# Twelve tiles of T written out in groups of five over six steps, and used again as raw weight tiles

## The chip, the cores and the metric

One Trainium2 chip; the kernel runs on one of its cores. The metric is the device time of one execution in microseconds (us), median of several executions. The kernel before took 1963.73 us (median of 3, 1962.33 to 1965.15).

## The reference

What is computed is one block with two branches on a sequence of 8192 rows of 448 channels. The first branch is a spectral mixer: layer norm, a Fourier transform over the 8192 rows, a small two-layer complex network on the frequencies in 4 blocks of 112 channels, and the inverse transform. The second is a gated feed-forward layer (GEGLU) of width 1792.

```python
mod = (_silu(c) @ w_mod).reshape(c.shape[0], 6, 1, -1)
sa, ca, ga, sb, cb, gb = (mod[:, 0], ..., mod[:, 5])
h = _layernorm(x, axis=-1) * (1 + ca) + sa
x = x + ga * _A_ref(h, A_w1, A_b1, A_w2, A_b2)      # rfft2, MLP, soft threshold, irfft2
h = _layernorm(x, axis=-1) * (1 + cb) + sb
x = x + gb * _B_ref(h, B_w_gate, B_w_up, B_w_down)  # (gelu(x@w_gate) * (x@w_up)) @ w_down
return x
```

## The kernel before

**Three stages.** The 8192 rows are taken as 128 x 64. In the first stage (0 to about 70 us) the 16 chunks of x are loaded into 16 tiles `xbuf[0..15]` (128 x 4 x 448, fp32), normalized and transformed over the 128 (`dft_a`, L198, line 200); the result T overwrites the chunk. In the second stage (70 to about 395 us) T is transformed over the 64, sent through the network and back. The third stage, to the end, does the last inverse step and the whole feed-forward layer; it is almost all matmuls.

**T goes through DRAM.** The second stage needs T with its rows arranged differently, so T is written to the DRAM tensor `td` and read back. T's 128 rows lie in an order in which every fourth partition belongs to one quarter: `store_t(ch, c)` (L258, DMA in line 261) writes quarter c of chunk ch, 32 partitions of 1792 numbers, 224 KB. Chunks 0 to 3 are written whole in the first stage, and so is quarter 0 of the other twelve (`CE` = 4 to 15). What is left is 3 quarters x 12 chunks = 36 stores of 224 KB. Quarter 0 serves units 0 to 7 of the second stage, quarter 1 units 8 to 15, quarter 2 units 16 to 23, quarter 3 the last eight.

**Units and steps.** The second stage has 32 units, one half of the channels (h) by one set of frequencies (bt) each, in a software pipeline. `step(i)` (L524) does, in the order of the code:
- `fetch_t` of unit i+2 (L316): two DMAs `tr<-td` of 224 KB (line 319) into a tile `tr` that has two buffers, and for every second unit a table `s<-cs` of 256 KB (line 325);
- the hooks "load" and "pe": other work that is hung on this step by `at(i, hook, ...)`, such as the weights' norm pass;
- `stage_s2` of unit i (L342): 24 short matmuls `ps<-s,th/tl` (lines 351 to 353), their results taken by ACT (`zh`, line 359) and DVE (`zl`, line 360);
- `split_t` of unit i+1 (L332): ACT casts `tr` to `th`, then POOL (DVE for units 0 and 1) makes `tl` of the difference (both by the helper `split`, lines 105 and 107);
- `stage_m2` of unit i-2 (L431, matmuls in lines 424 to 429, ACT `t`, eight DVE operations `y`), `stage_i1` of unit i-3 (L468, matmuls in lines 477 to 479, two DMAs `vd<-us` in line 487), `stage_m1` of unit i-1 (L380, matmuls in lines 397 to 402, ACT `hh`, DVE `hl`).

**What sets the order.** The whole stage is under a manual schedule: each engine runs its instructions in the order of the code. All these DMAs are issued by SP, one after the other; SP stops at the first whose semaphores are not yet there, and each DMA also waits for the one issued eight before it, so that at most eight are under way.

**Where the stores stand.** Twelve (quarter 1) follow the fetch of unit 1 (L583), twelve (quarter 2) stand behind `step(0)`, twelve (quarter 3) behind `step(1)` (L594 to L597). Then the pool `qp`, which holds the twelve tiles, is closed (L598).

**The norm pass.** From step 3 on, the feed-forward weights are loaded once to find their norms: `load_w` (three DMAs, 512 KB, lines 657 and 659), `load_m` (448 KB, line 767), `load_mod_row` (two DMAs of 392 KB, line 628). Their raw tiles come from `npool`, eight in rotation (`raw_tile`, L615), in memory that `qp` has given back.

Of the kernel before, what the change touches and what calls it, by code (L numbers as in the profile page):

```python
# [10 lines left out]
F32 = mybir.dt.float32  # L11
# [10 lines left out]
NA, NB, NG = 128, 64, 64  # L22
# [7 lines left out]
NC = 4  # L30
CE = 4
# [14 lines left out]
def spectral_geglu(ctx, tc, x, w1, b1, w2, b2, wg, wu, wd, cvec, wmod, cf1, cs2, cmi, cgm, out):  # L46
# [85 lines left out]
    qctx = ExitStack()  # L132
    qp = qctx.enter_context(tc.tile_pool(name="qp", bufs=1))
    with ExitStack() as actx:
# [5 lines left out]
        xbuf = [(ap if i < CE else qp).tile([128, 4, D], F32, name=f"xt{i}") for i in range(NB // 4)]  # L140
# [17 lines left out]
        q, y, t, nm, mu = (ap.tile([128, NB], F32, name=nm) for nm in ("q", "y", "t", "nm", "mu"))  # L158
# [99 lines left out]
        def store_t(ch, c=None):  # L258

            r = slice(0, 128) if c is None else slice(c, 128, NC)  # L260
            dma(td[r, ch * 4 : ch * 4 + 4], xts[ch][r])
# [10 lines left out]
        for g, bs in enumerate(groups):  # L272
# [5 lines left out]
            at = [pos[0] + 0.06] + [pos[i] + d for i in (1, 2, 3) for d in (0.03, 0.06)] + [pos[3] + 0.1]  # L278
            if g == 0:
                at = [t_stats[e] + 0.2] + [pos[0] + 0.03] * 7  # L280
# [23 lines left out]
    with ExitStack() as bctx:  # L304
# [11 lines left out]
        def fetch_t(h, bt):  # L316
            raw = bp1.tile([128, GB, HC], F32, tag="tr", name="tr", bufs=2)
            for ri in range(2):
                dma(
                    raw[ri * 64 : ri * 64 + 64],  # L320
                    td[rows(ri, bt), :, h * HC : (h + 1) * HC].rearrange("g b c -> b g c"),
                )
            if (h, bt) not in s2s:
                s2 = bp1.tile([128, GB, 2, 128], F16, tag="s2", name="s2", bufs=2)
                dma(s2, cs2[:, bt * GB : (bt + 1) * GB])
                if (0, bt) in units[:NS]:

                    s2s[(1, bt)] = s2
                s2s[(h, bt)] = s2
            trs[(h, bt)] = raw, s2s.pop((h, bt))  # L330

        def split_t(h, bt, el=G):  # L332
            raw, s2 = trs.pop((h, bt))
            th = bp1.tile([128, GB, HC], F16, tag="th", name="th", bufs=2)
            tl = bp1.tile([128, GB, HC], F16, tag="tl", name="tl", bufs=2)
            split(th, tl, raw, el=el)
            tts[(h, bt)] = th, tl, s2

        cnt = {"z": 0, "h": 0}
        ctx_u = {}  # L340

        def stage_s2(h, bt):  # L342
# [88 lines left out]
        def stage_m2(h, bt, p):  # L431
            hs = ctx_u[("h", h, bt)]
            ps = bank("pc", "pm2")
            for kk in range(2):
                mlp2(ps[:, kk * HC : (kk + 1) * HC], hs, kk, 2 * h + kk, slice(p * 128, p * 128 + 128))
            t = bp.tile([128, D], F32, tag="t", name="t", bufs=2)

            S.activation(t, ps[:, :D], AF.Relu, bias=nlam)  # L438
            drip()
            y = bp.tile([128, 2, 2, BS], F32, tag="y", name="y", bufs=2)  # L440
            pv = ps[:, :D].rearrange("p (k r c) -> p r k c", k=2, r=2)
            tv = t.rearrange("p (k r c) -> p r k c", k=2, r=2)
            for gi in range(2):
                for ri in range(2):
                    si = slice(gi * 64, gi * 64 + 64)
                    V.scalar_tensor_tensor(  # L446
                        y[ri * 64 : ri * 64 + 64, gi], pv[si, ri], LAM, tv[si, ri], op0=ALU.add, op1=ALU.min
                    )
            drip()
            if bt == 0 and p == 0:  # L450

                pn = bank("pb", "pn")
                for kk in range(2):
                    mlp2(pn[:2, kk * HC : (kk + 1) * HC], hs, kk, 2 * h + kk, slice(ZW - 2, ZW))
                tn = bp.tile([2, D], F32, tag="t", name="tn", bufs=2)
                V.tensor_scalar(tn, pn[:2, :D], LAM, -LAM, op0=ALU.min, op1=ALU.max)
                pnv = pn[:, :D].rearrange("p (k r c) -> p r k c", k=2, r=2)
                tnv = tn.rearrange("p (k r c) -> p r k c", k=2, r=2)
                V.tensor_tensor(y[64:65, 0], pnv[0:1, 0], tnv[0:1, 0], ALU.subtract)
            return y.rearrange("p g k c -> p g (k c)")  # L460

        def split_y(y, el=G):
            yh = bp.tile([128, 2, HC], F32R, tag="yh", name="yh", bufs=4)
            yl = bp.tile([128, 2, HC], F32R, tag="yl", name="yl", bufs=4)
            split(yh, yl, y, el=el)
            return yh, yl

        def stage_i1(h, bt):  # L468
            ys = ctx_u.pop(("y", h, bt))
            us = bp.tile([128, GB, HC], F32, tag="us", name="us", bufs=2)  # L470
            for p in range(GB // 2):
                yh, yl = ys[p]
                ps = bank("pd", "pi1")
                parts = [(0, 0, 1), (1, 1, 2)] if bt == 0 and p == 0 else [(1, 0, 2)]
                for m, lo, hi in parts:
                    o = ps[:, lo * HC : hi * HC]
                    T.matmul(o, mih[:, m, :], yh[:, lo:hi], start=True, stop=False)
                    T.matmul(o, mih[:, m, :], yl[:, lo:hi], start=False, stop=False)
                    T.matmul(o, mil[:, m, :], yh[:, lo:hi], start=False, stop=True)
                out = riders.pop()(ps) if riders and p else None  # L480
                S.copy(us[:, 2 * p : 2 * p + 2, :], ps[:, :D].rearrange("p (g c) -> p g c", g=2))
                if out:
                    out()
            if (h, bt) in units[-2:]:
                to_v(bt, us)
            for ro in range(2):
                dma(
                    vd[h, :, ro * 64 + bt * GB : ro * 64 + (bt + 1) * GB],
                    us[ro * 64 : ro * 64 + 64],
                )  # L490
# [30 lines left out]
        def at(i, hook, fn, *args):  # L521
            side.setdefault((i, hook), []).append((fn, args))

        def step(i):  # L524
            def hook(name):
                for fn, args in side.get((i, name), []):
                    fn(*args)

            if i + 2 < nu:
                fetch_t(*units[i + 2])  # L530
            hook("load")
            hook("pe")
            if i < nu:
                stage_s2(*units[i])
            if i + 1 < nu:
                split_t(*units[i + 1], el=V if i < 1 else G)
            hook("act")
            m2 = 0 <= i - 2 < nu
            if m2:
                y0 = stage_m2(*units[i - 2], 0)  # L540
                y = stage_m2(*units[i - 2], 1)
                ys = [split_y(y0)]
            if 0 <= i - 3 < nu:
                stage_i1(*units[i - 3])
            if m2:
                ctx_u[("y",) + units[i - 2]] = ys + [split_y(y)]
                del ctx_u[("h",) + units[i - 2]]
            hook("dve")
            if 0 <= i - 1 < nu:
                stage_m1(*units[i - 1])  # L550
            hook("pool")
# [28 lines left out]
        mod_row0(1)  # L580
        mod_row0(0)
        fetch_t(*units[1])
        for ch in range(CE, NB // 4):  # L583
            store_t(ch, 1)

        zh = [bp1.tile([113, 2, ZW], F32R, name=f"zh{i}") for i in range(4)]
        hh_ = [bp1.tile([113, 2, ZW], F32R, name=f"hh{i}") for i in range(4)]
# [3 lines left out]
        split_t(*units[0], el=V)  # L591
        lctx.close()
        bp = bctx.enter_context(tc.tile_pool(name="bp", bufs=1, side="right"))
        for i in range(2):  # L594
            step(i)
            for ch in range(CE, NB // 4):
                store_t(ch, 2 + i)  # L597
        qctx.close()  # L598


        def pow2(s, bnd, p=15):

# [10 lines left out]
            raws[key] = fn(pool, *args)  # L613

        def raw_tile(pool):  # L615
            return pool.tile([128, 4, 256], F32, tag="raw", name="raw", bufs=8 if pool is npool else 4)

        def load_mod_row(pool, q):
            out = []
            for hh in range(2):  # L620
                if pool is None:
                    wm = bp1.tile([128, GB, HC], F32, tag="tr", name="tr", bufs=2)[:112]
                elif callable(pool):
                    wm = pool().rearrange("p q c -> p (q c)")[:112, : 4 * HC].rearrange("p (q c) -> p q c", q=4)
                else:
                    wm = raw_tile(pool)[:112, :, :HC]
                c0 = q * D + hh * HC
                dma(wm, wmod[:, c0 : c0 + HC].rearrange("(k p) c -> p k c", p=112))
                out.append(wm)
            return out  # L630
# [160 lines left out]
        npool = nctx.enter_context(tc.tile_pool(name="npool", bufs=1))  # L791
# [15 lines left out]
        at(11, "dve", row_scales)  # L807
        at(16, "pe", scales1)
        at(16, "pe", scales2)
        for i in range(2, 17):  # L810
            step(i)
        nctx.close()

        wpool = ctx.enter_context(tc.tile_pool(name="wpool", bufs=1))
        wh = wpool.tile([128, 4, 2 * F], F16, name="wh")
# [513 lines left out]
```

## Time and profile before

| | |
|---|---|
| median of the runs | 1963.73 us |
| the profiled execution, own time | 1967.95 us |
| its span on the core | 1966.2 us |
| mean granted TensorE clock | 0.988 |
| busy: PE / DVE / ACT / POOL | 98% / 56% / 40% / 59% |
| DMA, mean over the span | 83 GB/s |

One slice of the page's second part is 49 us. The first five slices moved 347, 293, 246, 238 and 221 GB/s, the slices from the eleventh on some 43 GB/s: transfers are heavy in the first two stages and light afterwards. The row of the granted clock has 9s throughout but for an 8 in the second and third slices and around the start of the third stage.

In the rows of a timeline the first two numbers are the start and the duration in us, a bracket at the end is the idle time of the engine before the instruction and who ended it. "SPq" is SP's queue: the duration of a row there is that of the issuing, not of the transfer.

### The profile page before, as it was taken

The page shows a single profiled execution, that of the slowest core. Times are in us where ns is not written, and L with a number is a line of the kernel's source. Part 1 is how long each engine was busy: PE and PEld are TensorE (multiplying, and loading weights), DVE is VectorE, ACT ScalarE, POOL GpSimd, SP SyncE. Part 2 cuts the span into 40 slices and gives each one's busy share as a digit, 9 for nine tenths or more (in the row PEclk, how much of TensorE's full clock was granted, in tenths as well). Part 3 has the DMA queues.
Part 4 walks back from the last instruction along what each step waited for, and adds up shares of the span by engine and source line. Part 5 has one row for each costly group of instructions (what it writes and reads, how often), then busy time and mean ns, then how long its engine had stood idle before and what let it go on. Part 6 is the DMA issues. An engine that isn't in the chain of part 4 may idle for free.

```text
span 1966.2 us, 43631 instructions
## 1 busy us (share of the span) xinstructions
PE 1921.5 (98%) x17668; PEld 1707.7 (87%) x17668; DVE 1105.6 (56%) x2340; ACT 792.6 (40%) x1345; POOL 1163.0 (59%) x1470
## 2 busy tenths in 40 slices
PE   7899999889999999999999999999999999999998
PEld 3599999778888988888888888888889888888898
DVE  8557788775555555555555555555555555555533
ACT  5567888643233333333333333333333333333322
POOL 3146755345666666666666666666666666666644
PEclk9889999989999999999999999999999999999999
DMA  9888867642111111111111111111111111111000
GB/s 347 293 246 238 221 181 200 160 143 64 43 43 43 43 49 46 43 43 43 42 43 43 42 43 43 43 44 43 43 44 43 43 44 43 44 43 43 22 16 20
DMA packets 168750, 163.35 MB, mean 83 GB/s; under 512 B 87328, under 2 KB 147364, under 8 KB 168548
## 3 DMA queue, kind: packets, MB, share of 16 engines
q1 hardware_dynamic: 168532, 160.56, 28.3%
q8 instruction: 138, 2.26, 0.5%
q14 instruction: 64, 0.52, 0.1%
q10 hardware_dynamic: 16, 0.01, 0.0%
HBM read 97.47 MB, written 47.25 MB: 74 GB/s over the span
## 4 chain that ended last, share of the span: by engine, by line
PE 85%; DVE 5%; ACT 4%; issue 2%; DMA 2%; POOL 1%; SPq 1%; ACTq 0%; DVEq 0%; POOLq 0%
PE pgu L1051 51%; PE pdn L1119 8%; PE pdn L1117 8%; PE pdn L1118 8%; DVE y L446 3%; PE ps L200 2%; PE pi L951 1%; ACT th L105 1%; ACT zh L359 1%; ACT hh L414 1%; DMA tr<-td 1%; PE psm L636 1%; ACT t L438 1%; PE pi L949 1%; PE pi L950 1%
## 5 line engine op out<-in xcount | busy, mean ns | idle before, releaser
L1051 PE MATMUL pgu<-nt,wh 128*128 128x256 f16 x6272 | 836.2, 274 | 0.0
L1051 PEld LDWEIGHTS <-wh 128*128 128x128 f16 x6272 | 603.8, 98 | 99.3 <-issue 30.7
L1087 ACT ACTIVATE gel<-pgu,dg 128x256 f32<-128x256 f32 x448 | 200.2, 472 | 799.8 <-PE pgu L1051 762.7
L1051 PE MATMUL pgu<-nt,wl 128*128 128x256 f16 (+1 forms) x3584 | 503.4, 273 | 6.0 <-ACT nt L1044 3.2
L1119 PE MATMUL pdn<-wd,ac 128*128 128x224 f16 x1568 | 406.1, 259 | 0.2 <-DVE ac L1110 0.2
L1117 PE MATMUL pdn<-wd,ac 128*128 128x224 f16 x1568 | 406.1, 259 | 0.0
L1118 PE MATMUL pdn<-wd,ac 128*128 128x224 f16 x1568 | 406.1, 259 | 0.0
L1098 POOL TENSOR_TENSOR x<-x 128x128 f32<-128x128 f32 x223 | 240.7, 1079 | 266.8 <-DVE x L1092 266.8
L1110 DVE SCALAR_TENSOR_TENSOR ac<-x,sa_act,ac 128x896 f16<-128x896 f32 (+1 forms) x225 | 308.2, 1370 | 83.6 <-ACT ac L1109 83.6
L1051 PEld LDWEIGHTS <-wl 128*128 128x128 f16 (+1 forms) x3584 | 298.4, 97 | 63.9 <-issue 30.1
L1092 DVE TENSOR_TENSOR x<-pgu,gel 128x256 f32<-128x256 f32 x448 | 179.5, 418 | 283.4 <-ACT gel L1087 282.7
L1109 ACT ACTIVATE ac<-x,sa_act 128x896 f16<-128x896 f32 (+1 forms) x225 | 232.9, 1035 | 53.3 <-POOL x L1101 51.2
L1154 POOL TENSOR_TENSOR o<-u,p 128x224 f32<-128x224 f32 x32 | 21.1, 660 | 292.1 <-DVE u L1153 292.1
L1099 POOL TENSOR_TENSOR x<-x 128x128 f32<-128x128 f32 x223 | 158.5, 711 | 17.5
L1119 PEld LDWEIGHTS <-ac 128*128 128x128 f16 x1568 | 153.4, 98 | 0.5 <-DVE ac L1110 0.5
L1117 PEld LDWEIGHTS <-ac 128*128 128x128 f16 x1568 | 153.4, 98 | 0.4
L1118 PEld LDWEIGHTS <-ac 128*128 128x128 f16 x1568 | 153.4, 98 | 0.4
L446 DVE SCALAR_TENSOR_TENSOR y<-pm,t 64x224 f32<-64x224 f32 x256 | 99.5, 389 | 48.0 <-ACT t L438 44.0
L107 POOL TENSOR_TENSOR yl<-y,yh 128x448 fp32r<-128x448 f32 x63 | 78.8, 1251 | 77.5 <-ACT yh L105 66.5
L1100 POOL TENSOR_TENSOR x<-x 128x128 f32<-128x128 f32 x223 | 114.1, 512 | 0.0
L1101 POOL TENSOR_TENSOR x<-x 128x128 f32<-128x128 f32 x223 | 108.3, 486 | 0.0
L107 POOL TENSOR_TENSOR tl<-tr,th 128x896 f16<-128x896 f32 x30 | 57.2, 1908 | 78.0 <-ACT th L105 75.7
(281 smaller groups left out, 2761.5 us busy)
## 6 DMA issues: line engine op xcount, KB each, us to landing
tr<-td SPq DMA_DIRECT2D x64, 224.0 KB, 4.2
vd<-us SPq DMA_DIRECT2D x64, 224.0 KB, 3.1
xx<-in_A_x SPq DMA_DIRECT2D x32, 448.0 KB, 3.3
v<-vd SPq DMA_DIRECT2D x63, 224.0 KB, 2.9
out<-x SPq DMA_DIRECT2D x31, 448.0 KB, 2.9
xt<-in_A_x SPq DMA_DIRECT2D x15, 896.0 KB, 13.4
td<-xt SPq DMA_DIRECT2D x48, 224.0 KB, 3.8
nt<-pk SPq DMA_TRANSPOSE x480, 2.3
```

The source lines that it names most:

```text
L107: (el or V).tensor_tensor(lo, src, h, ALU.subtract)
L446: V.scalar_tensor_tensor(y[ri * 64 : ri * 64 + 64, gi], pv[si, ri], LAM, tv[si, ri], op0=ALU.add, op1=ALU.min)
L1051: T.matmul(pgu[i, t, q][:, pr * H : (pr + 1) * H], w[rows, tw, f0 : f0 + 128], nts[i][rows, tn, :], start=start, stop=stop, skip_group_che ...
L1087: S.activation(gl, ps[:, :H], AF.Gelu_apprx_tanh, scale=dg)
L1092: V.tensor_tensor(dst, ps[:, H : 2 * H].rearrange("p (b c) -> p b c", b=2), gl.rearrange("p (b c) -> p b c", b=2), ALU.mult)
L1098: e.tensor_tensor(s1, a21, a22, ALU.add)
L1099: e.tensor_tensor(s2, s1, a11, ALU.subtract)
L1109: S.activation(ac[:, 0, k], x[:, k], AF.Copy, scale=sc)
L1110: V.scalar_tensor_tensor(ac[:, 1, k], x[:, k], sc, ac[:, 0, k], op0=ALU.mult, op1=ALU.subtract)
L1117: T.matmul(ps, ac[:, 0, ka], wds[t][:, 0, kb], start=t == 0, stop=False)
L1118: T.matmul(ps, ac[:, 0, ka], wds[t][:, 1, kb], start=False, stop=False)
L1119: T.matmul(ps, ac[:, 1, ka], wds[t][:, 0, kb], start=False, stop=t == NP - 1)
```

## The change

The 36 stores are put into one list, chunk by chunk: quarters 1, 2 and 3 of chunk 4, then of chunk 5, and so on. Six of them are issued behind the fetch of unit 1. Of the other thirty, five are hung on each of the steps 0 to 5, as the last of the hook "load", behind the step's fetch and behind the loads of the norm pass. A chunk is done when its third quarter is written, so that its tile is free for other use early; the raw tiles of the norm pass are now views of the tiles `xbuf[4..11]` (the first 1024 of their 1792 columns), eight in rotation as before. The pool `qp` stays open until the norm pass is over.

```diff
-        for ch in range(CE, NB // 4):
-            store_t(ch, 1)
+
+        late = [(ch, c) for ch in range(CE, NB // 4) for c in range(1, NC)]
+
+        def store_late(n):
+            for ch, c in late[:n]:
+                store_t(ch, c)
+            del late[:n]
+
+        store_late(6)
...
-        for i in range(2):
-            step(i)
-            for ch in range(CE, NB // 4):
-                store_t(ch, 2 + i)
-        qctx.close()
...
         def raw_tile(pool):
-            return pool.tile([128, 4, 256], F32, tag="raw", name="raw", bufs=8 if pool is npool else 4)
+            if pool is npool:
+
+                t = xbuf[CE + cnt["raw"] % 8].rearrange("p t c -> p (t c)")
+                cnt["raw"] += 1
+                return t[:, :1024].rearrange("p (t c) -> p t c", t=4)
+            return pool.tile([128, 4, 256], F32, tag="raw", name="raw", bufs=4)
...
-        for i in range(2, 17):
+        for i in range(6):
+            at(i, "load", store_late, 5)
+        for i in range(17):
             step(i)
+        assert not late
         nctx.close()
+        qctx.close()
```

The order on the other engines stays as it was; only SP's changes. The tiles `xt_116` to `xt_127` in its rows are the chunks 4 to 15, x2 or x3 is the number of like DMAs in a row. Before, SP has these rows at the end of the first twelve stores, with the fetch of unit 2 behind them and the next twelve starting:

```order
L261 DMA td<-xt_125 32x1792
L261 DMA td<-xt_126 32x1792
L261 DMA td<-xt_127 32x1792
L319 DMA tr<-td 64x4x224 x2
L325 DMA s_837<-cs 128x1024
L261 DMA td<-xt_116 32x1792
L261 DMA td<-xt_117 32x1792
```

With the change, SP has these rows from the fetch of unit 1 to that of unit 4, the stores of the steps 0 and 1 among them:

```order
L319 DMA tr<-td 64x4x224 x2
L261 DMA td<-xt_116 32x1792 x3
L261 DMA td<-xt_117 32x1792 x3
L319 DMA tr<-td 64x4x224 x2
L325 DMA s_837<-cs 128x1024
L261 DMA td<-xt_118 32x1792 x3
L261 DMA td<-xt_119 32x1792 x2
L319 DMA tr<-td 64x4x224 x2
L261 DMA td<-xt_119 32x1792
L261 DMA td<-xt_120 32x1792 x3
L261 DMA td<-xt_121 32x1792
L319 DMA tr<-td 64x4x224 x2
```

The fetch of unit 2 thus stands behind 6 stores instead of 12, that of unit 3 behind 11 instead of 24, that of unit 4 behind 16 instead of 36.

The second place is SP's step 4, from the stores `vd<-us` of step 3 on. Before:

```order
L487 DMA vd<-us 64x896 x2
L319 DMA tr<-td 64x4x224 x2
L325 DMA s_1237<-cs 128x1024
L628 DMA raw<-in_w_mod 112x4x224 x2
L657 DMA raw<-in_B_w_up 128x3x256
L659 DMA raw<-in_B_w_up 64x256 x2
L767 DMA raw<-in_B_w_down 128x2x448
L487 DMA vd<-us 64x896 x2
```

With the change, where the raw tiles are `xt_117` to `xt_120`:

```order
L487 DMA vd<-us 64x896 x2
L319 DMA tr<-td 64x4x224 x2
L325 DMA s_1225<-cs 128x1024
L634 DMA xt_117<-in_w_mod 112x4x224
L634 DMA xt_118<-in_w_mod 112x4x224
L663 DMA xt_119<-in_B_w_up 128x3x256
L665 DMA xt_119<-in_B_w_up 64x256 x2
L773 DMA xt_120<-in_B_w_down 128x2x448
L261 DMA td<-xt_124 32x1792
L261 DMA td<-xt_125 32x1792 x3
L261 DMA td<-xt_126 32x1792
L487 DMA vd<-us 64x896 x2
```

Five stores have come between the loads of step 4 and its two `vd<-us`; steps 3 and 5 are changed in the same way. The last store of quarter 1 stands in step 5, and the fetch of unit 8, which reads it, in step 6.

More of the change, by code (lines that the diff above doesn't have):

```diff
@@ L337, in split_t @@
             tts[(h, bt)] = th, tl, s2
-        cnt = {"z": 0, "h": 0}
+        cnt = {"z": 0, "h": 0, "raw": 0}
         ctx_u = {}
```

## The prediction

> **What bounds the kernel now.** The page's first part says which engine is full:
>
> ```profile
> span 1966.2 us, 43631 instructions
> ...
> PE 1921.5 (98%) x17668; PEld 1707.7 (87%) x17668; DVE 1105.6 (56%) x2340; ACT 792.6 (40%) x1345; POOL 1163.0 (59%) x1470
> ```
>
> The table of windows shows that the third stage is full by itself:
>
> ```profile
> 400.00:1966.00 1566.00, 1553.04 (x14778) 1385.51 (x14776) 813.79 (x1607) 515.99 (x850) 979.82 (x1265) 0.99 0.16 44
> ```
>
> 1553 of 1566 us: no transfer holds PE there. A change to the second stage can only move the start of that stretch, so the question is by how much the second stage ends earlier or later. I read that from the stage's own waits, first on ACT, which casts what SP has fetched:
>
> ```profile
> 88.22 0.69 ACT L359 ACTIVATE zh<-ps,ca 112x512 fp32r<-112x512 f32 x1 [0.59 <-PE ps L353]
> 90.72 0.94 ACT L105 CAST th<-tr 128x896 f16<-128x896 f32 x1 [1.80 <-DMA tr<-td]
> 100.32 0.94 ACT L105 CAST th<-tr 128x896 f16<-128x896 f32 x1 [4.43 <-DMA tr<-td]
> 110.19 0.94 ACT L105 CAST th<-tr 128x896 f16<-128x896 f32 x1 [2.40 <-DMA tr<-td]
> 147.91 0.93 ACT L105 CAST th<-tr 128x896 f16<-128x896 f32 x1
> ```
>
> These are rows of ACT's timeline. The casts `th` at 90.72, 100.32 and 110.19 are those of units 2, 3 and 4; each waited for its fetch, 1.80, 4.43 and 2.40 us. The one at 147.91 (unit 8) waited for nothing, and the trace has no later wait of a cast for its fetch. Why the three are late stands in SP's timeline:
>
> ```profile
> 76.69 8.77 SPq L261 DMA_DIRECT2D td<-xt  x12
> 85.58 1.31 SPq L319 DMA_DIRECT2D tr<-td  x2
> 87.57 7.91 SPq L261 DMA_DIRECT2D td<-xt  x12
> 95.58 1.30 SPq L319 DMA_DIRECT2D tr<-td  x2
> 96.93 8.16 SPq L261 DMA_DIRECT2D td<-xt  x12
> 105.19 1.30 SPq L319 DMA_DIRECT2D tr<-td  x2
> 114.86 1.12 SPq L487 DMA_DIRECT2D vd<-us  x2
> ```
>
> Each of these three fetches goes out right behind twelve stores, which take 7.9 to 8.8 us to issue, and its cast starts 5.1, 4.7 and 5.0 us after the first issue. So it is SP's order that delays units 2 to 4, and from 110.19 on nothing of it is left. What the delay costs PE is the next view, PE's and POOL's timelines from the start of `stage_s2` of unit 2 (91.71) to that of unit 4 (116.47):
>
> ```profile
> 91.71 0.26 PE L351 MATMUL ps<-s,th 128*112 128x128 f16 x1
> 91.79 1.89 POOL L107 TENSOR_TENSOR tl<-tr,th 128x896 f16<-128x896 f32 x1 [37.16 <-ACT th L105]
> 93.73 0.26 PE L353 MATMUL ps<-s,tl 128*112 128x128 f16 x1 [1.70 <-POOL tl L107]
> 94.97 0.35 PE L424 MATMUL pm<-w2h,hh 113*128 113x224 f32 x1
> 97.73 0.28 PE L397 MATMUL pm<-zh,w1h 113*112 113x256 f32 x1
> 100.49 0.28 PE L402 MATMUL pm<-zh,w1l 112*112 112x256 f32 x1
> 101.31 0.26 PE L351 MATMUL ps<-s,th 128*112 128x128 f16 x1 [0.54 <-ACT th L105]
> 103.27 0.35 PE L353 MATMUL ps<-s,tl 128*112 128x128 f16 x1 [1.64 <-POOL tl L107]
> 106.20 0.56 PE L424 MATMUL pm<-w2h,hh 113*128 113x224 f32 x1 [0.34 <-ACT hh L414]
> 111.76 0.60 PE L477 MATMUL pi<-yh,mih 128*128 128x448 f32 x1
> 113.58 0.28 PE L397 MATMUL pm<-zh,w1h 113*112 113x256 f32 x1
> 116.47 0.22 PE L351 MATMUL ps<-s,th 128*112 128x128 f16 x1
> ```
>
> PE stood before lines 353 and 351 for the halves `th` and `tl` of a late unit (1.70, 0.54, 1.64 us) and briefly for `hh`. And the same work takes twice as long behind the second gap: 24 matmuls of lines 424 to 429 fill 94.97 to 97.73 (2.76 us) for unit 0, but 106.20 to 111.76 (5.56 us) for unit 1. The windows say why; the third number from the end is the granted clock:
>
> ```profile
> 95.00:100.00 5.00, 5.00 (x46) 5.00 (x45) 1.42 (x2) 0.89 (x2) 0.00 (x0) 1.00 0.95 292
> 105.00:110.00 5.00, 4.66 (x25) 4.24 (x24) 2.66 (x5) 2.71 (x5) 1.37 (x2) 0.50 0.92 261
> ```
>
> Half the clock, in a stretch that follows PE's idling. So the late fetches are paid twice: in waiting and in slow matmuls.
>
> **The change part by part.**
>
> *The fetches go out earlier.* Unit 2: 6 stores instead of 12 ahead of it, so about half of 8.77 us; issue at about 81.1, cast possible at 81.1 + 5.1 = 86.2. ACT is not free until 88.22 + 0.69 = 88.9, so the wait of 1.80 us is gone and ACT's own order bounds what is left. Unit 3: the fetch before it and its table take about 2 us, five stores at 7.91 / 12 = 0.66 us take 3.3; issue at 86.4, cast possible at 91.1, against 100.32. Unit 4: 1.3 + 5 x 0.68 = 4.7 us later, 91.1, or when POOL has let go of unit 2's `tr` buffer (about 91.9); cast possible at 96.9, against 110.19. All three waits go, and what is late next is PE itself.
>
> *PE's path from 91.7.* With no wait and the clock of the 95 to 100 row, the pieces from 91.71 to 116.47 are: `s2` of unit 2 0.2 + (94.97 - 93.73) = 1.44; `m2` of unit 0 2.76; `m1` of unit 1 (97.73 to about 100.6) 2.88; `s2` of unit 3 1.44 again; `m2` of unit 1 2.76; `i1` of unit 0 about 1.27 (its 1.82 us from 111.76 on were partly at the low clock); `m1` of unit 2 (113.58 to 116.47) 2.89. Sum 15.44 us, where 24.76 were spent: of the 9.3 between them 4.7 is clock (`s2` of unit 3 106.20 - 0.34 - 103.27 = 2.59 for 1.24; `m2` 5.56 for 2.76; `i1` 1.82 for 1.27) and 4.6 waiting. Not all the waiting can go. Unit 2's `tl` comes no earlier than 88.9 + 0.94 for the cast + 2.0 for POOL = 91.9, 0.2 after PE asks; `hh` and `hl` of unit 1 stand behind two casts of `y` and the eight operations of DVE, and by their present spacing come 0.3 to 0.8 us after `s2` of unit 3 ends. I leave 0.8 us of waiting: **the gain is 9.3 - 0.8 = 8.5 us**, reached at `stage_s2` of unit 4, which starts at about 108.0 instead of 116.47. PE has no gap behind that point in the trace, so the lead is kept unless something new makes it wait.
>
> *The stores now lie among other transfers.* 16 of the 36 are issued by the end of step 1, ten more by the end of step 3, and steps 4 and 5 hold ten that used to be gone by 105. The DMAs are the same in number, size and tiles' rotation; the last fetch that needs them in time is unit 8's, issued in step 6 behind the last of quarter 1. With the lead, step 3's `vd<-us` goes out at 114.86 - 8.5 = 106.3. From there to the fetch of unit 8 SP issues, by the shapes in its rows, three pairs `vd` and two pairs `tr` (5 x 448 KB), one table (256), two weight tiles (1024), the pair of w_mod (784), one tile of w_down (448) and ten stores (2240): 6992 KB, 7.16 MB. The rates that the trace has for such traffic, last number of each row:
>
> ```profile
> 87.60:95.50 7.90, 6.11 (x59) 5.75 (x57) 3.03 (x5) 3.61 (x7) 1.89 (x1) 0.90 1.03 371
> 107.00:116.00 9.00, 9.00 (x48) 8.82 (x49) 4.90 (x11) 5.31 (x10) 3.38 (x3) 0.66 0.79 188
> 116.00:125.40 9.40, 9.40 (x95) 9.17 (x94) 5.92 (x12) 7.28 (x13) 4.21 (x4) 1.00 1.03 250
> 154.70:163.50 8.80, 8.80 (x83) 8.69 (x82) 7.03 (x20) 7.23 (x14) 8.03 (x24) 1.00 1.03 304
> 163.50:175.30 11.80, 11.80 (x111) 11.41 (x110) 7.93 (x20) 7.74 (x16) 5.47 (x20) 1.00 0.68 172
> ```
>
> 371 GB/s is nearly all stores; 250 and 304 are loads of the norm pass with the DMA engines full (share 1.03); 188 and 172 are windows in which the share, 0.79 and 0.68, shows that less was asked for. I take stores at 371 (2.29 MB, 6.2 us) and the rest at 250 (4.87 MB, 19.5 us): fetch at 106.3 + 25.7 = 132.0, cast possible 5.0 us later at 137.0. It is wanted at 147.91 - 8.5 = 139.4. So the stores are just hidden, with 2.4 us to spare (6 us at 304). The cover is the steps' own PE work; without it each us late is a us lost.
>
> [...]
>
> *The raw tiles and the pool.* Tiles, their rotation of eight and their readers are as before; the first loads, into chunks 4 to 8 in steps 3 and 4, stand at least one whole step behind the last store of their chunk, which in the trace is some 9 us against about 4 us from issue to landing. Costed at nothing; a wait there would be at most the rest of one such landing, 0 to 4 us, and would sit on SP, ahead of a fetch with that much slack.
>
> **The rivals.**
>
> *A. The mix is slower than I take it.* If stores between short-row loads bring the whole to 220 GB/s, between the 188 and 250 rows, 7.16 MB take 32.5 us, unit 8's cast is possible at 143.8, 4.4 us late, and the gain is 4.1. For it: the engines are full at 250 already. Against: 304 in a like window.
>
> *B. The clock stays low.* If the slow stretch comes all the same, only the waiting goes: 4.6 - 0.8 = 3.8 us. For it: PE still has gaps at 80 to 86, which the change doesn't touch, and short ones later. Against: the 1.70 us gap at 92 was followed by a full clock. [...]
>
> *C. Slower.* The lead is lost where 7.16 MB take more than 147.91 - 5.0 - 106.3 = 36.6 us, that is, below 196 GB/s. At the lowest row, 172, they take 41.6 us, unit 8's cast is 13.5 us late, and the kernel 5.0 us slower than before. Against: 172 and 188 were not the engines' limit.
>
> *D. No gain.* The early fetches wait for something else, such as the quarter's stores as a whole, and land where they did: 0. Against: only the 1.80, 4.43 and 2.40 us behind the batches.
>
> **How the numbers follow.** The profiled execution took 1967.95 us by its own time (span 1966.2), 4.2 above the median of the runs, 1963.73; 8.5 of 1967.95 is 0.43%, so the median becomes 1963.73 - 8.5 = **1955.2 us**. Chances: forecast 0.67 (1953.5 to 1957.5), A 0.15 (1959.6), B 0.09 (1959.9), C 0.04 (1968.7), D 0.05 (1963.7). The range runs from the whole 9.3 us and a little for the spread of the runs, 1953.3, to 1960.3, which takes in A and B. About 0.2%, 3.9 us, is what a measurement of this kernel can tell from no change; A and B lie at that line and are split there. Faster 0.81, same 0.15, slower 0.04.
>
> **What would show it.** Right: in ACT's timeline the casts of units 2, 3 and 4 at about 89, 94 and 102 with no wait for `tr<-td`; a clock of 1.00 in all windows from 90 on to 115; `stage_s2` of unit 4 at about 108; the third stage's first matmuls 8 to 9 us earlier. Rival A or C: a cast of units 7 to 9, or an operation on the raw tiles, waiting for its DMA, and SP's `vd<-us` of steps 4 and 5 issued more than 4 us behind `us`. B: matmuls of lines 424 to 429 at twice their time after 100. What would make me wrong altogether is a second stage that gives the lead back after step 6, where I have found no wait to take it.

## The result, and the profile after

| | median, us | runs |
|---|---|---|
| before | 1963.73 | 5 (1962.27 to 1965.15) |
| changed | 1953.71 | 5 (1950.90 to 1957.31) |

The ratio is 0.9949, interval 0.9936 to 0.9962: faster by 0.38 to 0.64%. Predicted were 1955.2 us and a range of 1953.3 to 1960.3.

First ACT's timeline of the changed kernel, with the rows of the casts of units 2, 3, 4 and 8, the making of `us` in step 4, and the square of a raw tile of the norm pass:

```profile
86.80 0.93 ACT L105 CAST th<-tr 128x896 f16<-128x896 f32 x1
...
91.87 0.93 ACT L105 CAST th<-tr 128x896 f16<-128x896 f32 x1
...
99.20 0.95 ACT L105 CAST th<-tr 128x896 f16<-128x896 f32 x1
...
111.94 0.96 ACT L481 COPY us<-pi 128x448 f32<-128x448 f32 x2
...
117.69 1.06 ACT L670 ACTIVATE sq<-xt 128x1024 bf16<-128x1024 f32 x1 [0.73 <-DMA xt<-in_B_w_up]
...
136.71 0.95 ACT L105 CAST th<-tr 128x896 f16<-128x896 f32 x1
```

None of these casts has a bracket any more: the waits of 1.80, 4.43 and 2.40 us are gone, and unit 8's cast, 11.2 us earlier than before, doesn't wait for the quarter that the stores now write later. New is the bracket of 0.73 us at line 670: a square that waits for its raw tile.

SP's timeline says why the casts are early, and how the stores fare afterwards:

```profile
74.54 3.82 SPq L261 DMA_DIRECT2D td<-xt  x6
78.90 1.31 SPq L319 DMA_DIRECT2D tr<-td  x2
80.90 4.16 SPq L261 DMA_DIRECT2D td<-xt  x5
85.17 1.31 SPq L319 DMA_DIRECT2D tr<-td  x2
86.53 3.34 SPq L261 DMA_DIRECT2D td<-xt  x5
89.96 1.31 SPq L319 DMA_DIRECT2D tr<-td  x2
...
103.89 1.11 SPq L487 DMA_DIRECT2D vd<-us  x2
...
111.05 6.20 SPq L261 DMA_DIRECT2D td<-xt  x5
117.35 1.17 SPq L487 DMA_DIRECT2D vd<-us  x2
...
127.84 1.28 SPq L319 DMA_DIRECT2D tr<-td  x2
```

The fetches of units 2, 3 and 4 go out at 78.90, 85.17 and 89.96 instead of 85.58, 95.58 and 105.19. Unit 8's goes out at 127.84. Step 4's five stores hold up what stands behind them: its `vd<-us` goes out at 117.35, 4.4 us after `us` is done (111.94 + 0.96 = 112.90); before, that DMA followed within 0.03 us (124.27 behind 124.24).

PE's timeline, from `stage_s2` of unit 2 to that of unit 4:

```profile
89.12 0.22 PE L351 MATMUL ps<-s,th 128*112 128x128 f16 x1
89.81 0.26 PE L353 MATMUL ps<-s,tl 128*112 128x128 f16 x1 [0.41 <-POOL tl L107]
91.06 0.35 PE L424 MATMUL pm<-w2h,hh 113*128 113x224 f32 x1
...
98.02 0.35 PE L424 MATMUL pm<-w2h,hh 113*128 113x224 f32 x1
101.02 0.38 PE L477 MATMUL pi<-yh,mih 128*128 128x448 f32 x1
...
105.13 0.22 PE L351 MATMUL ps<-s,th 128*112 128x128 f16 x1
```

The stretch takes 105.13 - 89.12 = 16.01 us instead of 24.76, and the 24 matmuls of unit 1 from line 424 on 101.02 - 98.02 = 3.00 instead of 5.56. The windows (the third number from the end is the granted clock, the last ones are the DMA share and GB/s) show the clock, and the rate from step 3's `vd<-us` to unit 8's fetch:

```profile
95.00:100.00 5.00, 5.00 (x55) 4.83 (x54) 3.83 (x8) 3.94 (x7) 2.30 (x2) 1.00 1.02 322
100.00:105.00 5.00, 5.00 (x40) 4.90 (x39) 3.44 (x9) 3.70 (x8) 3.35 (x3) 1.00 0.90 322
105.00:110.00 5.00, 5.00 (x55) 4.96 (x54) 3.02 (x5) 4.72 (x8) 2.59 (x2) 1.00 0.97 246
103.89:127.84 23.95, 23.95 (x230) 23.36 (x229) 14.86 (x31) 17.80 (x30) 12.47 (x12) 1.00 0.99 290
```

Full clock where before had 0.50 (105 to 110) and 0.66 (107 to 116), and PE busy throughout.

**How much of the difference is the change's.** The span fell from 1966.2 to 1952.6, by 13.6 us, which is more than the medians' 10.0. Three marks in the profile tell the change's part from the spread between executions: the first cast `th` (start of the second stage), unit 8's cast, and unit 31's, the last. Before and changed were each profiled twice (`b2_before_again`, `a2_after_again`):

| kernel | first cast, us | to unit 8's | to unit 31's | from there to the end of the span |
|---|---|---|---|---|
| before | 78.15 | 69.76 | 275.52 | 1612.5 |
| before again | 77.19 | 69.91 | 275.64 | 1607.7 |
| changed | 76.14 | 60.57 | 266.65 | 1609.8 |
| changed again | 77.16 | 60.15 | 266.29 | 1609.9 |

The second stage repeats to 0.4 us, and is 275.6 - 266.5 = **9.1 us** shorter; all of it is there by unit 8 (69.8 - 60.4 = 9.4) and stays. The start of the stage lies between 76.1 and 78.6 in all fourteen profiles of this study, and from the last cast on it varies by some 5 us, whatever the kernel. The other 4.5 us of the 13.6 are of these two kinds, which no run ties to the change.

### The profile page after: what moved, and what is told of

The parts are those of the page before. It is cut to its first block, busy times and chain, and to the rows that moved or that the text cites. A ratio compares the mean times of both kernels' runs of the same rounds, so it can differ in the third digit from the quotient of the medians.

```text
span 1952.6 us, 43627 instructions
## 1 busy us (share of the span) xinstructions
PE 1910.0 (98%) x17668; PEld 1700.3 (87%) x17668; DVE 1104.3 (57%) x2340; ACT 792.0 (41%) x1345; POOL 1162.4 (60%) x1470
## 4 chain that ended last, share of the span: by engine, by line
PE 85%; DVE 5%; ACT 3%; issue 2%; POOL 2%; SPq 1%; DMA 1%; ACTq 0%; DVEq 0%; POOLq 0%
PE pgu L1061 51%; PE pdn L1129 8%; PE pdn L1128 8%; PE pdn L1127 8%; DVE y L446 2%; PE ps L200 2%; PE pi L961 1%; PE psm L642 1%; PE pi L959 1%; PE pi L960 1%; DVE st L161 1%; POOL tl L107 0%; SPq L1031 0%; PE ps L351 0%; ACT zh L359 0%
```

## The experiments

"Marks" are the distances from the first cast as in the table above. Each ratio is to the kernel before, measured on the same chip. No kernel leaves out work of the computation; filler matmuls are overwritten by the ones behind them.

**The same kernels again.**

> The kernel before once more, for a second profile: how far the end of the first stage (first cast at 78.15 in the first profile) and the third stage (first gate matmul at 404.2 to the last end) move from one execution to the next. If both move by 1 to 3 us, the 2.0 and 2.6 us by which the changed kernel's profile is shorter there are spread between executions; if they come back within 0.3 us, they belong to the change.

> The changed kernel once more, timed beside the three below, for a second profile. From the first cast th to that of unit 8 the kernel before took 69.8 and 69.9 us in its two profiles, the changed one 60.6. If the gain sits there alone, this comes back within 0.5 us, while the first stage (76 to 78.5 us so far) and the third (1557.9 to 1562.0) stay where the kernel before has them, and the time is 9 to 10 us below the kernel before, 1953 to 1956 us.

Before again: a single run, 1962.33 us, marks in the table. Changed again: 1955.17 us (5 runs), ratio 0.9953 (0.9941 to 0.9966). The square of the first `w_up` tile waited longer this time, in ACT's timeline:

```profile
118.29 1.06 ACT L670 ACTIVATE sq<-xt 128x1024 bf16<-128x1024 f32 x1 [1.70 <-DMA xt<-in_B_w_up]
```

In the first profile of before it waited for nothing, in the second 1.22 us, so this wait is partly an old one.

**Which part of the change gains.** The stores in bunches of twelve again, with the new chunk order and the reuse of the tiles kept:

```diff
-        store_late(6)
+        store_late(12)
...
-        for i in range(6):
-            at(i, "load", store_late, 5)
+        for i in range(2):
+            at(i, "load", store_late, 12)
```

> The changed kernel, but its 36 stores again in three bunches of twelve (behind the fetch of unit 1, in step 0, in step 1), still chunk by chunk and with the raw tiles in the chunks' tiles. Theory (only the fetches' place behind the stores counts): the casts of units 2, 3 and 4 wait about 1.8, 4.4 and 2.4 us for tr again, the clock falls to 0.5 around units 1 to 2, stage_s2 of unit 4 starts some 9 us later after the first cast than in the changed kernel, and the time is that of the kernel before, 1962 to 1965 us. Rival (reusing the tiles, or the order by chunks, brings the gain): the time stays near 1954 us.

1964.75 us, ratio 0.9995 (0.9986 to 1.0003), marks 70.03 and 275.74: the whole gain is gone. ACT's timeline of this kernel has the waits of the kernel before, and its window the low clock:

```profile
91.31 0.94 ACT L105 CAST th<-tr 128x896 f16<-128x896 f32 x1 [2.00 <-DMA tr<-td]
...
100.66 0.94 ACT L105 CAST th<-tr 128x896 f16<-128x896 f32 x1 [4.17 <-DMA tr<-td]
...
111.17 0.94 ACT L105 CAST th<-tr 128x896 f16<-128x896 f32 x1 [3.04 <-DMA tr<-td]
```

```profile
105.00:110.00 5.00, 4.49 (x25) 4.06 (x24) 3.00 (x5) 2.70 (x5) 1.71 (x2) 0.50 0.88 263
```

Chunk order and reuse of the tiles by themselves bring or cost nothing that can be told; the spreading is the gain.

**Is the low clock the price of PE's idling?** In the kernel before, 40 matmuls with the identity fill PE's gap ahead of unit 3; the late fetches stay.

```diff
                 ps = bank("pa", "ps2")
+                if (h, bt) == units[3] and kk == 0:
+                    for _ in range(40):
+                        T.matmul(ps[:, :128], ident, ident, start=True, stop=True)
```

> The kernel before with 40 extra matmuls of the identity (128x128, overwritten afterwards) ahead of stage_s2 of unit 3, which fill 2.2 of the 2.7 us in which PE waits there; no fetch comes earlier. Theory (the low granted clock from 103 on is paid for by PE's idling): the clock stays at 1.00, lines 424 to 429 of unit 1 take 2.8 us instead of 5.6, and the kernel is 3.3 us faster than before, 1960.4 us (stage_s2 of unit 3 gains nothing, since hh of unit 1 comes at 105.6 anyway). Rival (the clock falls for another reason): lines 424 to 429 at 5.6 us, 1963.7 us.

The clock stays up, in the window in which the kernel before has 0.50, and the 24 matmuls from line 427 (424 before) take 108.51 - 105.23 = 3.28 us instead of 5.56:

```profile
105.00:110.00 5.00, 4.53 (x33) 4.24 (x34) 2.61 (x4) 3.16 (x6) 1.21 (x2) 1.00 0.98 233
```

```profile
105.23 0.37 PE L427 MATMUL pm<-w2h,hh 113*128 113x224 f32 x1 [1.40 <-ACT hh L417]
108.51 0.38 PE L480 MATMUL pi<-yh,mih 128*128 128x448 f32 x1
```

```profile
108.66 0.94 ACT L105 CAST th<-tr 128x896 f16<-128x896 f32 x1 [1.84 <-DMA tr<-td]
```

So it was PE's idling that brought the clock down here, and work in its place keeps it up. But the marks gain only 1.7 us (unit 8 68.11, last cast 273.90), half of what was expected, and the time, 1963.03 us with ratio 0.9991 (0.9982 to 1.0000), can't be told from before's. The rows say where the rest went. PE is quicker, but now stands 1.40 us for `hh` of unit 1 (0.34 in the kernel before), which ACT makes behind the late cast of unit 3; and unit 4's cast still waits 1.84 us for its fetch. So most of what the slow matmuls cost is time that a faster PE spends waiting, and the full clock alone saves little. No run takes away the waiting and leaves the clock low.

**How many stores fit where.** None in steps 0 to 2, ten in each of 3 to 5; and twelve behind unit 1's fetch, then four per step:

```diff
-        for i in range(6):
-            at(i, "load", store_late, 5)
+        for i in range(3, 6):
+            at(i, "load", store_late, 10)
```

> The changed kernel with no stores in steps 0 to 2 and ten instead of five in each of steps 3, 4 and 5. Theory (the stores there are hidden with about 4 us to spare: unit 8's fetch is issued at 127.8, its cast could start 5 us later and starts at 136.7): ten more stores, 2.29 MB, take 6 to 8 us more up to that fetch, so the casts of units 7 and 8 or the squares of the raw tiles wait for DMAs, and the kernel is 3 to 6 us slower than the changed one, 1957 to 1960 us. Rival (transfers there are hidden anyway, SP has much more room): no change, 1953 to 1955 us.

```diff
-        store_late(6)
+        store_late(12)
...
-            at(i, "load", store_late, 5)
+            at(i, "load", store_late, 4)
```

> The changed kernel with twelve stores instead of six ahead of the fetch of unit 2, and four instead of five in each of steps 0 to 5. Only unit 2's fetch is late again. Theory (each late fetch costs what PE waits for it): unit 2's cast waits 1.8 to 2.8 us, PE some 1.4 us longer for its tl, the clock stays full as it did behind that gap before, and the kernel is 1 to 2 us slower than the changed one (1955 to 1956 us). Rival (one gap of PE in these steps is enough to bring the clock down): 4 us or more slower, lines 424 to 429 at twice their time.

`e3_late_stores`: 1960.97 us, ratio 0.9979 (0.9971 to 0.9988), and a last cast 7.1 us later than in the changed kernel. SP's ten stores of step 4, then ACT behind them:

```profile
113.94 8.78 SPq L261 DMA_DIRECT2D td<-xt  x10
```

```profile
142.14 0.94 ACT L105 CAST th<-tr 128x896 f16<-128x896 f32 x1 [2.60 <-DMA tr<-td]
144.36 1.06 ACT L670 ACTIVATE sq<-xt 128x1024 bf16<-128x1024 f32 x1 [1.28 <-DMA xt<-in_B_w_up]
...
155.55 1.06 ACT L670 ACTIVATE sq<-xt 128x1024 bf16<-128x1024 f32 x1 [1.85 <-DMA xt<-in_B_w_gate]
```

Here unit 8's cast does wait, 2.60 us, and the squares behind it; the loss is the rival C of the prediction in small. In the first steps nothing more was to be had: from the first cast to unit 4's it is 23.09 us here with no stores at all in steps 0 to 2, 23.06 and 21.65 in the two profiles of the changed kernel.

`e4_twelve_first`: 1957.44 us, ratio 0.9967 (0.9955 to 0.9979), and marks some 2.3 us longer than the changed kernel's, a little more than expected. Unit 2's cast waits again, PE behind it for `tl`, and the window has the full clock (ACT, PE, windows):

```profile
88.95 0.94 ACT L105 CAST th<-tr 128x896 f16<-128x896 f32 x1 [1.83 <-DMA tr<-td]
```

```profile
91.97 0.26 PE L353 MATMUL ps<-s,tl 128*112 128x128 f16 x1 [1.71 <-POOL tl L107]
```

```profile
90.00:95.00 5.00, 3.29 (x41) 3.15 (x41) 2.71 (x4) 2.94 (x5) 1.89 (x1) 1.00 0.96 318
```

PE stood 1.71 us, once, and the clock stays at 1.00 from 90 on: this gap cost its own length and some 0.6 us more.

**Is there more at the stage's start?** `split_t` of unit 1 ahead of `stage_s2` of unit 0; and the same with 26 identity matmuls ahead of unit 0:

```diff
             hook("pe")
+            if i == 0:
+                split_t(*units[1], el=V)
             if i < nu:
                 stage_s2(*units[i])
-            if i + 1 < nu:
-                split_t(*units[i + 1], el=V if i < 1 else G)
+            if 0 < i < nu - 1:
+                split_t(*units[i + 1], el=G)
```

> The changed kernel with split_t of unit 1 moved ahead of stage_s2 of unit 0 in step 0, so that ACT casts unit 1 before it waits for unit 0's matmuls. With the fetches no longer late, ACT's own order is what PE waits for next (1.60 and 0.67 us ahead of unit 1's matmuls). Theory: stage_s2 of unit 1 follows that of unit 0 without a gap, and the second stage is 2 to 2.5 us shorter than in the changed kernel: 1951 to 1953 us. Rival (unit 1's fetch lands too late, or unit 0's zh is now late): no change, 1953 to 1956 us.

> As e6_split_first, with 26 matmuls of the identity (overwritten afterwards) ahead of the matmuls of unit 0, where PE waits for th and tl in the first cast's time. Theory (the low clock of steps 0 and 1 comes from the gaps around the first cast): stage_s2 of units 0 and 1 runs at the full clock and the second stage is 1 to 2.5 us shorter than in e6_split_first: 1949 to 1952 us. Rival (the fetches and casts of units 0 and 1 set the pace there anyway, or the clock falls all the same): as e6_split_first.

`e6_split_first`: 1952.51 us, ratio 0.9950 (0.9938 to 0.9963), marks 60.01 and 266.14, which is 0.1 to 0.6 us better than the two profiles of the changed kernel, not 2 to 2.5. Unit 1's cast now waits for its fetch:

```profile
80.12 0.94 ACT L105 CAST th<-tr 128x896 f16<-128x896 f32 x1 [1.93 <-DMA tr<-td]
```

`e8_split_and_fill`: 1954.24 us, ratio 0.9944 (0.9932 to 0.9957), marks 60.51 and 266.65. The clock between 75 and 90 rises (0.92, 0.74 and 1.00 in windows of 5 us, 0.80, 0.50 and 0.68 in `e6_split_first`), but then unit 2's cast waits for its fetch:

```profile
87.44 0.94 ACT L105 CAST th<-tr 128x896 f16<-128x896 f32 x1 [1.58 <-DMA tr<-td]
```

Neither gain is there at the end, though the start gets shorter: from the first cast to unit 4's `e6_split_first` takes 21.78 us, 1.3 less than the first profile of the changed kernel. But the second profile takes 21.65 without any edit, so what the edit did isn't shown. The clock between 80 and 85 was 0.91 in that second profile and 0.50 in the first, which is a likely reason for its quicker start (windows, first and second profile):

```profile
80.00:85.00 5.00, 2.73 (x23) 2.33 (x23) 2.60 (x3) 1.88 (x4) 0.00 (x0) 0.50 1.03 312
```

```profile
80.00:85.00 5.00, 2.59 (x35) 2.30 (x34) 2.52 (x4) 2.87 (x4) 0.00 (x0) 0.91 1.03 322
```

`e6_split_first` and the second profile had both lost most of that lead by unit 8; where, the next runs show. In `e8_split_and_fill` the fetches take it already: 22.46 us to unit 4.

**The new wait at line 670.** Two theories: step 4's five stores slow the `w_up` tile that is loaded there; or step 4's own loads ahead of it, the pair of `w_mod`. No stores in step 4; the same with the early `split_t`:

```diff
-        for i in range(6):
-            at(i, "load", store_late, 5)
+        for i, n in enumerate((7, 7, 6, 5, 0, 5)):
+            at(i, "load", store_late, n)
```

> The changed kernel with its 30 later stores dealt as 7, 7, 6, 5, 0, 5 over the steps 0 to 5 instead of five each, so that step 4, which has the most loads, has none. In the changed kernel's two profiles the square of unit-like raw tile n1 (w_up, loaded in step 4) waited 0.73 and 1.70 us for its DMA, and PE 0 and 0.8 us in step 6 for it. Theory (step 4's transfers are the one place where the spread stores still cost something): SP issues step 4's vd at its time, 3 us earlier, the waits on raw tiles from step 5 on go, unit 7's cast comes 11.8 us after unit 6's (11.9 and 12.9 in the two profiles), and the second stage is 0 to 1 us shorter; the time cannot be told from the changed kernel's, 1952 to 1956 us. n1 itself is loaded ahead of step 4's stores, so if its wait stays, it is step 3's stores or the pair of w_mod that delay it.

> e6_split_first with the same dealing of stores (7, 7, 6, 5, 0, 5). e6 had unit 6's cast 38.6 us after the first cast (39.9 and 38.5 in the two profiles of the changed kernel) and unit 7's 51.2 (51.8 and 51.4). Theory (what e6 wins ahead of step 5 is given back there, because step 5 waits for raw tiles): unit 7's cast at 50.4 after the first, and the second stage up to 1 us shorter than in e6. Rival (step 5 is held by something else): unit 7's cast at 51.2 again.

`e10_lighter_step4`: 1954.45 us, ratio 0.9954 (0.9942 to 0.9967); the last cast is 3.3 us later than in the changed kernel. The wait grew, PE stood behind it, and the clock fell (ACT, PE, windows):

```profile
120.00 1.06 ACT L670 ACTIVATE sq<-xt 128x1024 bf16<-128x1024 f32 x1 [2.50 <-DMA xt<-in_B_w_up]
```

```profile
124.42 4.98 PE L642 MATMUL psm<-xt,cs 112*128 112x224 f32 x16 [1.64 <-ACT us L481]
```

```profile
120.00:124.00 4.00, 2.78 (x24) 2.56 (x22) 2.23 (x6) 2.73 (x5) 0.00 (x0) 1.00 1.11 284
124.00:128.00 4.00, 3.58 (x11) 3.26 (x12) 3.26 (x6) 2.35 (x5) 3.41 (x4) 0.60 1.03 376
```

`e9_split_lighter`: 1952.63 us, ratio 0.9951 (0.9938 to 0.9965), the wait 2.58 us, last cast 267.58. So the wait doesn't need step 4's stores, which stand behind that load on SP. But the dealing also puts five more stores ahead of the load, 31 instead of 26, and the load goes out 34.4 us after the first cast instead of 32.0 (SP's timelines, changed kernel and `e10_lighter_step4`):

```profile
108.11 0.49 SPq L663 DMA_DIRECT2D xt<-in_B_w_up  x1
```

```profile
111.02 0.49 SPq L663 DMA_DIRECT2D xt<-in_B_w_up  x1
```

The two kernels also differ in what the wait cost. In `e9_split_lighter` PE stood 1.72 us, about as long as in `e10_lighter_step4` (1.64), ahead of the same 16 matmuls, but they took 3.29 us instead of 4.98, which is what they take in the changed kernel at a clock of 1.00 (122.12 to 125.41):

```profile
123.52 3.29 PE L644 MATMUL psm<-xt,cs 112*128 112x224 f32 x16 [1.72 <-ACT us L481]
```

Next, the `w_mod` pair two steps earlier; and that with the early `split_t`:

```diff
-        at(4, "load", pre, npool, "cb", load_mod_row, 4)
+        at(2, "load", pre, npool, "cb", load_mod_row, 4)
```

> The changed kernel with the load of the pair of w_mod for cb_r (784 KB) in step 2 instead of step 4, nothing else. It stands ahead of n1's load (w_up) in step 4 now, and n1's square waited 0.73, 1.70, 1.4 and 2.5 us for it in the kernels so far, whether step 4 held stores or not. Theory (n1 is late because of step 4's own loads, once the steps have the lead): n1's square does not wait, unit 7's cast comes 11.8 us after unit 6's (11.9 and 12.9 in the changed kernel), the second stage is 0 to 1 us shorter; the time cannot be told from the changed kernel's, 1952 to 1956 us. Rival (it is the traffic as a whole up to there): the wait stays above 0.7 us.

> e6_split_first with the same load moved to step 2. e6 had unit 6's cast 1.3 us earlier than the first profile of the changed kernel, counted from the first cast, and unit 8's only 0.6. Theory: without n1's wait the lead stays; unit 8's cast at 59.1 after the first (60.0 in e6, 60.6 and 60.2 in the changed kernel), and 0.5 to 1.5 us less than the changed kernel: 1951 to 1954 us. Rival: 60.0 again.

`e11_mod_row_early`: the square starts without a wait:

```profile
117.27 1.06 ACT L670 ACTIVATE sq<-xt 128x1024 bf16<-128x1024 f32 x1
```

So the loads ahead of it were what it waited for. The time is 1954.81 us, ratio 0.9955 (0.9942 to 0.9967), marks 60.45 and 266.44: no gain. From unit 6's cast to unit 7's it takes 11.78 us here, and 11.92 and 12.88 in the two profiles of the changed kernel. So in the first of them the wait (0.73 us) had cover; in the second (1.70 us) it cost 1.1 of the 1.4 us that the quicker start had brought. `e12_split_mod_row`: 1952.10 us, ratio 0.9948 (0.9934 to 0.9961), marks 58.89 and 264.94, the shortest second stage of all, 1.5 us below the changed kernel's: it has the quick start (21.50 us to unit 4) and keeps it (11.77 from unit 6 to 7). That is one profile. Its time can't be told from the changed kernel's 0.9949.

## Why the prediction was right, and where it was not

**Fetches and waits: right.** Casts of units 2 to 4 were forecast at about 89, 94 and 102 without a wait; they stand at 86.80, 91.87 and 99.20, of which 2.0 us is the earlier start of this execution's second stage. `e1_bunched` shows that the place of the stores alone does it, `e4_twelve_first` that unit 2's wait comes back with twelve stores ahead of it.

**PE's path: right, and its size nearly.** Forecast was a gain of 8.5 us from unit 2 to unit 4; it is 24.76 - 16.01 = 8.75. Of the 0.8 us of waiting that was left in the sum, 16.01 - 15.44 = 0.57 is left. The second profiles give 24.32 - 15.57, again 8.75. The rest lies ahead of unit 2, where the sum has no term: from the first cast to `stage_s2` of unit 2 it is 89.12 - 76.14 = 12.98 us instead of 91.71 - 78.15 = 13.56, another 0.6. That part isn't shown to be the change's, since the same stretch took 12.02 us in the changed kernel's second profile and 13.58 in `e11_mod_row_early`. With it, 9.3 by unit 4, of which 9.1 reaches the end of the stage. The medians' 10.0 us, near the favourable end of the range, has the spread of the runs in it: 9.1 us is 0.46%, inside the interval of 0.38 to 0.64%.

**Clock and waiting: the split was wrong.** The prediction parted the 9.3 us into 4.7 of clock and 4.6 of waiting, and priced rival B at 3.8 by taking one away. `e2_before_filled` brought the clock back and gained 1.7 us in the marks. The terms share time: with the fetches still late (unit 4's cast waited 1.84 us there), the faster PE stood 1.40 us for `hh` instead of 0.34. The sum was right because the change removes both, not because its two terms were.

**Stores hidden: right, with more to spare.** Step 3's `vd<-us` to unit 8's fetch took 127.84 - 103.89 = 23.95 us, forecast 25.7; 7.16 MB in that time are 299 GB/s by the shapes (290 in the window's row), between the rates of 371 and 250 that were taken. With the forecast's 5.0 us from issue to cast, unit 8's could start at 132.8 and was wanted at 136.71: 3.9 us to spare instead of 2.4. `e3_late_stores` goes beyond that and loses what the prediction calls the cover.

**"Costed at nothing": right for the tiles, incomplete as a step.** SP's waits show no load into a raw tile that stops for a store `td<-xt`, and `e1_bunched` has the reuse and the chunk order at no cost that can be told. But the prediction looked only at unit 8's fetch for what the lead would meet, and there was a second: the first `w_up` tile, whose square waited 0.73 and 1.70 us. `e11_mod_row_early` puts that down to step 4's own loads ahead of it; in the marks it cost 0.1 us in the first profile and 1.1 in the second, in the medians nothing that can be told. That the wait was longest without stores in step 4 (2.50 and 2.58 us) fits the load's later issue there; no run separates the two. So both signs that the prediction names for A or C can be seen, a raw tile that waits and, in step 4, a `vd<-us` 4.4 us behind `us` (3.3 in step 5). The loss that goes with A or C didn't come: as signs of it they were too weak.

**The rivals.** A (220 GB/s) and C (under 196) fell with the measured 299 GB/s (290 in the window's row); B with the clock of 1.00 behind 90; D with the fetches that go out 6.7 to 15.2 us earlier. `e2_before_filled` speaks against B as well: with PE's gap ahead of unit 3 filled, the clock was 1.00 between 105 and 110, where the kernel before had 0.50.

## What to carry to other kernels

Where one queue issues all transfers in order, as SP does here, put the next consumer's fetch ahead of a batch of writes, and deal the writes over steps that have room, up to the first fetch that reads them. Here gaps of PE (0.54 and 1.64 us) were paid twice, in waiting and in a clock of 0.50, but the two overlapped: to bring back the clock alone gained 1.7 us of the 3.3 expected. Price the removal of both together, not one by one. After a gain, look for each transfer that the lead will catch up with, not only for the one whose data was moved.

## What the hardware showed that was not expected

The granted clock fell after short gaps: to 0.50 in the kernel before, where 0.54 and 1.64 us lie close together, and to 0.60 in `e10_lighter_step4` right behind a gap of 1.64 us. Yet a gap of 1.71 us in `e4_twelve_first` left it at 1.00, and behind one of 1.72 us in `e9_split_lighter` the same 16 matmuls took 3.29 us, not the 4.98 of the clock of 0.60. What tells them apart no run shows, and one and the same kernel had 0.50 and 0.91 between 80 and 85 in two executions: a profile's loss by the clock may not be there in the next. And the clock came back late: in the kernel before it was 0.66 on average in the window from 107 to 116, in which PE was busy for all of the 9.00 us.
